# Turning q' and k' of three pairs by halves of the tokens, in two row tiles

## The chip, the core and the metric

The kernel runs on one core of one Trainium2 chip, in one launch. The metric is the device time of an execution in microseconds (us). Profiles show one execution by engine: PE is TensorE (PEld its weight loads), DVE is VectorE, ACT is ScalarE, POOL is GpSimd and SP is SyncE, which here issues DMAs alone. "L428" is line 428 of the kernel.

## What is computed

A gated linear recurrence for 4 batches, 8 heads, 768 tokens and a head width of 48, and behind it a feed-forward layer with GELU over all 3072 tokens:

```python
state = np.zeros((B, H, D, D), dtype=np.float32)
for t in range(S):
    state = alpha[:, :, t, :, None] * state + np.einsum('bhd,bhe->bhde', k[:, :, t], v[:, :, t])
    y[:, :, t] = np.einsum('bhd,bhde->bhe', q[:, :, t], state)
x = np.ascontiguousarray(y.transpose(0, 2, 1, 3)).reshape(B * S, H * D)      # 3072 x 384
h = x @ w_in                                                                  # 384 x 2048
g = 0.5 * h * (1.0 + np.tanh(c * (h + 0.044715 * h * h * h)))
out = g @ w_out                                                               # 2048 x 384
```

## The kernel before

**Tiles.** The tokens are cut into 6 chunks of 128. A unit is one batch in one chunk; two batches of a chunk make a pair, so there are 12 pairs, numbered 0 to 11 in the code (`m`). Within a chunk the recurrence becomes matrix products. ScalarE takes the logarithm of alpha (`ln`), TensorE sums it along the tokens (`cum`, L378 and L380), ScalarE takes exponentials (`b`, `binv`, `bend`, L401 and L407), and VectorE scales q and k with them to q' and k' (`qp` and `kp`, L418), in tiles with tokens on the 128 partitions and 2 units x 8 heads x 64 columns (48 of them used).

**The turn.** The attention product needs q' and k' with features on the partitions, so they have to be turned. For pairs 7 to 11 a DMA does this (`TURN_QK`); for pairs 0 to 6 TensorE does it, by a product with the identity: `turn` (L428) takes two heads at a time, 128 tokens x 128 features, as weights, and writes 128 features x 128 tokens to PSUM. For pairs 2 to 6 one task `t` turns one unit, 4 products for q' and 4 for k', into one bank (`yk`, of which there are two), and one task `ev` copies that bank, 1024 elements of each partition, into the tile `qkT` (`turned`, L446). VectorE does the copy, or, for pairs 0 to 3 (`EV_ACT`), ScalarE where the planner finds it sooner free. In `qkT` the 128 tokens of a unit lie side by side for each operand and head pair.

**Behind the turn.** `attn` (L489) multiplies k' and q' head by head, with 64 of the 128 rows for each head: the two heads of a head pair use the two halves of the rows, and write to two banks. From pair 3 on it does both units of a pair at once. VectorE masks the result (`mask`, L496). `kv` (L506) makes the chunk's share of the state from k' and v, into a `yk` bank; VectorE adds and scales it (L528 and L531). `y` (L543 and L546) adds what the state and the chunk itself give, into a `yk` bank; `x` (L553) copies it, `tx` (L560) turns it, and `xe` (L564, VectorE) copies it into `xT`. From pair 6 on a DMA turns x.

**The feed-forward layer.** For each pair TensorE does eight groups `l1` of six products with `w_in` (hT, L572), ScalarE takes the GELU of each group (L578), and for each unit TensorE does four groups `l2` of four products with `w_out` (acc, L591), whose sum is copied (`ot`, L603) and stored (L616). hT and acc take turns in four banks of PSUM, `ff`; cum and the attention share two more, `ca`.

**The order.** `Scheduler` makes a task of each of these steps. It holds a planned cost for each kind (`W`), a priority, the tasks that must be done before, and the buffers that it takes (`take`) with those who must be done before a buffer is free again. Up to about 49 us the order is written out by hand (`FIRST`); from there on the planner puts in, engine by engine, the task of the best priority among those that can start soonest. Where TensorE would idle by the plan, before a given time (`until`), it puts in products with zeros (`fill`). Each engine then runs its queue in that order and waits on semaphores.

Of the kernel before, what the change touches and what calls it, by code (L numbers as in the profile page):

```python
# [5 lines left out]
BF16 = mybir.dt.bfloat16  # L6
# [10 lines left out]
    cum=530, cum_packed=1500, t8=450, t4=225, attn=340, kv=170, inter=170, intra=205, tx=168, l1_4=655, l1_2=340, l2=655,  # L17
    qk2=910, qk1=500, ev8=650, ev4=350, mask=640, st=1090, st0=545, end=110, attn2=590, vb=320, vb_act=480, ring=1300, ring_issue=670, out=2050, lead=600, receipt=1400, receipt_hw=1000, xc=520, xe=330, ot=540,
    ev8_act=960, ev4_act=520, xc_act=450, xe_act=450, ot_act=450,
    strip=1700, cast=1900, weight=2080, dma=2100, issue=1100, wissue=760, sp=100, store=2600, turn=1250, landed=2200, xbar_qk=1500, xbar_x=1000, late_x=2500, late_qk=1200, piece=330, late_k=1500, piece_issue=450, begin=620, cast_0=1300, share=1200, cast_1=1900, ln_packed=1040, cold=380, fill=216, zero=1100,  # L20
)
COST = {
    ("ACT", "b"): (385, 135), ("ACT", "binv"): (385, 135), ("ACT", "ev"): (600, 40), ("ACT", "gelu"): (510, 110),
# [23 lines left out]
class Scheduler:  # L47
# [16 lines left out]
    def order(self):  # L64
        free = {e: 0 for e in LAT}
        taken = {tag: [] for tag in self.bufs}
        table, wire, xbar, head, out = LN_EXP, 0, 0, 0, []
        left = {e: sorted((t for t in self.tasks if e in t.cost), key=lambda t: t.prio) for e in LAT}

        def given(tag):  # L70

            n, at = len(taken[tag]) - self.bufs[tag], 0
            for u in taken[tag][n] if n >= 0 else ():
                if u.done is None:
                    return None
                at = max(at, u.done)
            return at

        def ready(t, inorder=True):
            if inorder and t.stream not in (None, head):  # L80
                return None
            at = 0
            for d in t.deps:
                if d.done is None:
                    return None
                at = max(at, d.done)
            for tag, _ in t.takes:
                g = given(tag)
                if g is None:
                    return None  # L90
                at = max(at, g)
            return at

        def put(t, at, e):
            nonlocal wire, xbar
            for tag, users in t.takes:
                taken[tag].append(users)
            cost, lat = COST.get((e, t.kind), (t.cost[e], LAT[e])) if fixed and not 300 <= t.prio < 10000 else (t.cost[e], LAT[e])
            t.start, t.end, t.engine, t.load = at, at + cost, e, None
            free[e] = t.end  # L100
            t.done = t.end + lat
            if t.name in self.landed:
                t.done = self.landed[t.name]
                if e != "SP":
                    wire = t.done - W["receipt"]
            elif t.land is not None:
                wire = max(wire, t.end + W["lead"]) + t.land
                t.done = wire + W["receipt_hw" if e == "SP" else "receipt"]
            if t.kind in ("turn", "store"):
                xbar = t.done = max(xbar, t.end + W["landed"] - t.xbar) + t.xbar  # L110
                t.done += t.late
            out.append(t)

        def go(at, e, t):
            nonlocal table, head
            if e == "PE" and not fixed and self.fill and at < self.until and at - free[e] > 300:
                g = given("ff")
                n = int((at - max(free[e], g if g is not None else at) - 60) * 0.95 // W["fill"])
                if n > 0:
                    f = Task("fill", {"PE": n * W["fill"]}, 0, self.fill(n))  # L120
                    put(f.take("ff", f), max(free[e], g), e)
            put(t, at, e)
            if t.table not in (None, table):
                table = t.load = t.table
            for q in t.cost:
                left[q].remove(t)
            if t.stream is not None:
                head = min((x.stream for x in left["PE"] if x.stream is not None), default=None)

        fixed = True  # L130
        for step in self.first:
            e, name = step.split(":")
            if name[:5] == "fill.":
                n = int(name[5:])
                f = Task("fill", {"PE": n * W["fill"]}, 0, self.fill(n))
                at = given("ff")
                assert at is not None, "no bank for idle products"
                put(f.take("ff", f), max(free["PE"], at), "PE")
                continue
            e, t = {"P": "PE", "V": "DVE", "A": "ACT", "G": "POOL", "S": "SP"}[e], self.named[name]  # L140
            at = ready(t, False)
            assert at is not None, f"{name} can't go yet"
            go(max(at, free[e] + (W["table"] if t.table not in (None, table) else 0)), e, t)
        fixed = False
        while any(left.values()):
            best = None
            for e in LAT:
# [12 lines left out]
            assert best is not None, "no task can go on"  # L160
            go(*best)
        return out
# [9 lines left out]
class _Kernel:  # L172
# [25 lines left out]
        A:b2.1 A:binv2.1 P:t2.0 P:l20.3 V:kp2.1 A:ev2.0 V:qp2.1 P:l20.10 A:bend2.1 P:attn2.0 P:t2.1 V:mask2.1 P:l20.7 A:ev2.1 V:mask2.0 P:l20.14 A:ln3.0  # L198
        P:attn2.1 P:y2.0 V:mask2.2 P:l20.13 V:mask2.3 P:l20.12 V:x2.0 P:cum3.0 A:ot0.0 V:ot0.1 P:y2.1 A:ot0.2 S:store0.0 S:store0.1 P:tx2.0 P:l20.11 A:x2.1
        S:store0.2 V:xe2.0 A:b3.0 P:tx2.1 P:l20.15 V:xe2.1 A:binv3.0 V:end2.0 P:l12.0 V:ot0.3 A:bend3.0 P:l12.1 V:qp3.0 S:store0.3 P:kv2.0 P:l12.2 V:st2.0  # L200
        A:gelu2.0 P:l12.3 V:end3.0 V:kp3.0 A:gelu2.1 P:l12.4 A:gelu2.2 P:t3.0 A:gelu2.3 P:t3.1 A:gelu2.4 V:ev3.0 P:l12.5
    """.split()
    LANDED = {"load.0": 2800, "load.1": 3400, "load.2": 4400, "load.3": 5000, "load.4": 6000, "load.5": 7300, "load.12": 10100, "load.6": 9200, "load.7":
# [7 lines left out]
    TURN_QK, TURN_X = (7, 8, 9, 10, 11), (6, 7, 8, 9, 10, 11)  # L211

    EV_ACT = (0, 1, 2, 3)

    AT_FF, SINGLE = {0: (1,), 1: (), 2: ()}, (0, 1, 2)

# [221 lines left out]
    def turned(self, u, i, which):  # L438
# [7 lines left out]
            self.copy(e)(t, ps)  # L446
        return emit

    def turn_back(self, u, i):

        def emit(e):
            ps = u["k_ps", i] = self.tile("yk", [self.C, self.H // 2, self.C], BF16, "k_ps")
            for p in range(self.H // 2):
                self.nc.tensor.transpose(ps[:, p], u["T"][:, 1, i, p], self.ident)
        return emit
# [161 lines left out]


    def tasks(self):
        s = self.s = Scheduler(self.BUFS, self.fill, 60000, self.FIRST, self.LANDED)  # L620
        B, NCH = self.B, self.NCH
        NP = B // 2
        self.p = {(c, i): {} for c in range(NCH) for i in range(NP)}
# [3 lines left out]
        loads, n, gate, held = {}, 0, [], {}  # L627
# [26 lines left out]
        for step in self.LOADS:  # L654
            if step[0] == "v":
                rows(int(step[1:]), "v")
            elif step[:4] == "gate":
                r, m, j = step[4:].split()
# [12 lines left out]
        for m, (c, i) in enumerate(pairs):  # L671
# [43 lines left out]
            if m in self.TURN_QK:  # L715
                tq = [s.add("turn", {"SP": W["turn"]}, P + 10, self.turn_dma(u, n), d, xbar=W["xbar_qk"], late=W["late_qk"] * (m < 8)) for n, d in (("q", qp), ("k", kp))]
                owner, turned = tq[0], tq
            backs = []
            vin = [loads["v", m, j] for j in range(2)]
            if m in self.NARROW:  # L720
# [2 lines left out]
                end = s.add("end", {"DVE": W["end"]}, P + 16, self.ends(u), be)  # L723
            for j in range(2):
                o, k = P + 10 + 3 * j, kp[j]
                if m not in self.TURN_QK:
                    turned = []
                    o -= 3 * u["packed"]
                    for which in ("q", "k") if early else ("qk",):
                        n = 4 * len(which)  # L730
                        cost = {"DVE": W[f"ev{n}"] + 270 * u["packed"]}
                        if m in self.EV_ACT:
                            cost["ACT"] = W[f"ev{n}_act"] + 80 * u["packed"]
                        t1 = s.add("t", {"PE": W[f"t{n}"]}, o, self.turn(u, j, which),
                                   ([qp[j]] if "q" in which else []) + ([k] if "k" in which else []))
                        turned.append(s.add("ev", cost, o, self.turned(u, j, which), [t1]))
                        t1.take("yk", turned[-1])
                        tq.append(t1)
                        if len(tq) == 1:
                            owner = turned[0]  # L740
# [12 lines left out]
            for j in range(2):  # L753
# [6 lines left out]
                    xe = tx = s.add("turn", {"SP": W["turn"]}, P + 22 + j, self.turn_x_dma(u, j, c, b), [xc], xbar=W["xbar_x"], late=W["late_x"] * (m < 6))  # L760
                else:
                    tx = s.add("tx", {"PE": W["tx"]}, P + 22 + j, self.turn_x(u, j), [xc])
                    xe = s.add("xe", {"DVE": W["xe"]}, P + 22 + j, self.turned_x(u, j, c, b), [tx])
                    tx.take("yk", xe)
                y.take("yk", xc)
                xc.take("x", tx)
# [38 lines left out]
        n = 0  # L805
# [115 lines left out]
```

## Time and profile before

| | |
|---|---|
| three runs, median (lowest to highest) | 177.44 us (176.88 to 177.53) |
| profiled execution, span from the first to the last instruction | 175.3 us |
| TensorE busy | 170.4 us (97%), 1845 products |
| TensorE weight loads busy | 135.4 us (77%) |
| VectorE busy | 96.8 us (55%) |
| ScalarE busy | 128.9 us (74%) |
| GpSimd busy (issue of loads) | 57.7 us (33%) |
| granted TensorE clock | 1.000 |
| turns of q' and k' by TensorE (L428) | 112 products, 5.4 us for q', 5.4 us for k' |

Of the profiled execution the profile tells the span, from its first to its last instruction, and no other time. The runs lie about 2 us above it. Busy times are unions of the times in which an engine worked; a product's time in the profile holds its way through the array, so products overlap, and what a product adds to the queue is the distance from its start to the next one's. The turns of pairs 3, 4 and 5 stand at 47.3, 59.0 and 73.0 us after the span's start.

### The profile page before, as it was taken

The page shows a single profiled execution, that of the slowest core. Times are in us where ns is not written, and L with a number is a line of the kernel's source. Part 1 is how long each engine was busy: PE and PEld are TensorE (multiplying, and loading weights), DVE is VectorE, ACT ScalarE, POOL GpSimd, SP SyncE. Part 2 cuts the span into 40 slices and gives each one's busy share as a digit, 9 for nine tenths or more (in the row PEclk, how much of TensorE's full clock was granted, in tenths as well). Part 3 has the DMA queues.
Part 4 walks back from the last instruction along what each step waited for, and adds up shares of the span by engine and source line. Part 5 has one row for each costly group of instructions (what it writes and reads, how often), then busy time and mean ns, then how long its engine had stood idle before and what let it go on. Part 6 is the DMA issues. An engine that isn't in the chain of part 4 may idle for free.

```text
span 175.3 us, 4440 instructions
## 1 busy us (share of the span) xinstructions
PE 170.4 (97%) x1845; PEld 135.4 (77%) x1845; DVE 96.8 (55%) x192; ACT 128.9 (74%) x213; POOL 57.7 (33%) x64
## 2 busy tenths in 40 slices
PE   7989999999999999999999999999999999999993
PEld 2667999667987896797798698698697697796973
DVE  6499920356888993795598897495426405000000
ACT  4677999666968668768788967977987984481941
POOL 2496348977645776576720000000000000000000
PEclk9999999999999999999999999999999999999999
DMA  4999999999999999999999992271271360401102
GB/s 138 307 262 224 210 243 238 246 205 207 249 273 204 242 256 220 217 226 199 200 264 224 200 136 80 54 172 52 47 187 28 90 165 4 115 20 49 45 0 90
DMA packets 49620, 28.86 MB, mean 165 GB/s; under 512 B 37696, under 2 KB 46016, under 8 KB 49600
## 3 DMA queue, kind: packets, MB, share of 16 engines
q0 software_dynamic: 26464, 17.70, 60.8%
q1 hardware_dynamic: 22592, 10.49, 24.8%
q10 hardware_dynamic: 544, 0.39, 0.8%
q8 instruction: 14, 0.23, 0.6%
q14 instruction: 6, 0.05, 0.1%
HBM read 25.17 MB, written 4.72 MB: 170 GB/s over the span
## 4 chain that ended last, share of the span: by engine, by line
PE 90%; DMA 6%; DVE 1%; issue 0%; ACT 0%; SPq 0%; POOL 0%
PE hT L572 36%; PE acc L591 36%; DMA v<-in_v_dram 4%; PE at L489 4%; PE qkT_ps L428 3%; PE yps L546 3%; PE kv L506 2%; PE yps L543 2%; DMA a<-in_alpha_dram 2%; PE cum L378 2%; PE xT_ps L560 1%; PE cum L380 1%; SPq L305 0%; ACT qkT L446 0%; DVE vb L389 0%
## 5 line engine op out<-in xcount | busy, mean ns | idle before, releaser
L572 PE MATMUL hT<-xT,w_in 128*128 128x256 bf16 x576 | 69.4, 273 | 0.0
L578 ACT ACTIVATE gT<-hT 128x512 bf16<-128x512 f32 x96 | 56.3, 600 | 17.7 <-PE hT L572 14.2
L591 PE MATMUL acc<-w_out,gT 128*128 128x384 bf16 (+3 forms) x416 | 69.0, 313 | 0.0
L572 PEld LDWEIGHTS <-w_in 128*128 128x128 bf16 x576 | 61.1, 114 | 1.6
L591 PEld LDWEIGHTS <-gT 128*128 128x128 bf16 x416 | 36.9, 98 | 19.2
L496 DVE TENSOR_TENSOR atm<-at,ut 128x512 bf16<-128x512 f32 x48 | 30.1, 681 | 12.7 <-PE at L489 12.6
L418 DVE TENSOR_TENSOR qp<-q,b 128x768 bf16<-128x768 f32 (+1 forms) x15 | 11.9, 794 | 14.0 <-ACT b L407 11.7
L418 DVE TENSOR_TENSOR kp<-k,binv 128x768 bf16<-128x768 f32 (+1 forms) x15 | 11.9, 791 | 10.6 <-ACT binv L407 10.6
L603 ACT COPY ot<-acc 128x384 f32<-128x384 f32 (+3 forms) x17 | 7.4, 439 | 13.0 <-PE acc L591 12.9
L308 POOL DMA_DIRECT2D k<-in_k_dram x11 | 12.2, 1107 | 6.6 <-DVE atm L496 3.0
L308 POOL DMA_DIRECT2D vb<-in_v_dram x11 | 12.1, 1102 | 6.7 <-PE hT L572 1.7
L308 POOL DMA_DIRECT2D q<-in_q_dram x11 | 12.2, 1109 | 6.1 <-DVE atm L496 1.3
L308 POOL DMA_DIRECT2D a<-in_alpha_dram x11 | 12.2, 1114 | 5.9 <-DMA w_in<-in_moe_w_in_dram 1.3
L407 ACT ACTIVATE b<-cum 128x768 bf16<-128x768 f32 (+1 forms) x15 | 10.3, 683 | 3.6 <-PE cum L380 2.3
L280 ACT ACT_TABLE_LOAD x9 | 11.5, 1283 | 0.9 <-PEq L905 0.7
L578 ACT ACT_TABLE_LOAD x9 | 11.5, 1283 | 0.2
L407 ACT ACTIVATE binv<-cum 128x768 bf16<-128x768 f32 (+1 forms) x15 | 10.2, 681 | 0.1
L528 DVE TENSOR_TENSOR stmp<-kv,st 128x384 f32<-128x384 f32 x16 | 8.8, 552 | 2.0 <-PE kv L506 2.0
L553 DVE CAST x<-yps 128x384 bf16<-128x384 f32 x12 | 6.7, 556 | 4.7 <-PE yps L546 4.7
L531 DVE TENSOR_TENSOR st<-stmp,ends 128x384 bf16<-128x384 f32 x16 | 8.9, 558 | 0.6
L446 ACT COPY qkT<-qkT_ps 128x512 bf16<-128x512 bf16 (+1 forms) x9 | 6.5, 728 | 3.7 <-PE qkT_ps L428 3.5
L546 PE MATMUL yps<-vb,atm 128*128 128x48 bf16 x192 | 8.7, 183 | 0.4 <-DVE vb L389 0.4
(65 smaller groups left out, 156.7 us busy)
## 6 DMA issues: line engine op xcount, KB each, us to landing
out_dram<-ot SPq DMA_DIRECT2D x19, 192.0 KB, 5.2
a<-in_alpha_dram POOLq DMA_DIRECT2D x9, 384.0 KB, 12.5
q<-in_q_dram POOLq DMA_DIRECT2D x9, 384.0 KB, 11.6
k<-in_k_dram POOLq DMA_DIRECT2D x9, 384.0 KB, 11.7
vb<-in_v_dram POOLq DMA_DIRECT2D x9, 192.0 KB, 11.6
w_in<-in_moe_w_in_dram POOLq DMA_DIRECT2D x4, 384.0 KB, 9.3
w_out<-in_moe_w_out_dram POOLq DMA_DIRECT2D x4, 384.0 KB, 11.1
out_dram<-ot SPq DMA_DIRECT2D x9, 96.0 KB, 1.8
```

Of the source, the lines that this page charges most:

```text
L280: nc.scalar.add_instruction(mybir.InstLoadActFuncSet(name=nc.get_next_instruction_name(), act_func_set_id=i, engine=mybir.EngineType.Activ ...
L308: dma(u[t][:, lo:hi].rearrange("t b h d -> t (b h) d"), src.rearrange("b h s d -> s (b h) d")[c * C:(c + 1) * C])
L407: self.nc.scalar.activation(u[n].rearrange("t i h d -> t i (h d)")[:, lo:hi], cum, AF.Exp, scale=1.0 if n == "b" else -1.0)
L418: self.nc.vector.tensor_tensor(out, rows, b, op=ALU.mult)
L496: self.nc.vector.tensor_tensor(u["atm", i][:, o], u["at", i][o], self.ut[:, None, :].to_broadcast([self.C, self.H // 2, self.C]), op=ALU.mult)
L528: nc.vector.tensor_tensor(s, acc, old, op=ALU.add)
L531: nc.vector.tensor_tensor(new.rearrange("f p (o d) -> f (p o) d", o=2), acc.rearrange("f p (o d) -> f (p o) d", o=2), ends, op=ALU.mult)
L546: nc.tensor.matmul(y[:, h, :], u["atm", i][:, h % 2, h // 2, :], u["vb"][:, i, h, :], start=c == 0, stop=True, skip_group_check=True)
L572: self.nc.tensor.matmul(h[:, s], w_in[:, j, nt % 4 + s], self.xT[c % self.NX][:, j, lo:hi].rearrange("p g t -> p (g t)"), start=j == 0, st ...
L578: return lambda e: self.nc.scalar.activation(self.gT[c % self.NG][:, nt:nt + 2, lo * self.C:hi * self.C], f.pop(("h", c, lo, nt)), AF.Gelu ...
L591: self.nc.tensor.matmul(f["acc", c, b][:, lo:hi], self.gT[c % self.NG][:, nt, b * self.C:(b + 1) * self.C], self.w_out[:, nt, lo:hi], star ...
L603: self.copy(e)(f["ot", c, b][:, sl], f["acc", c, b] if half is None else f["acc", c, b, half][:, sl])
```

## The change

For pairs 3, 4 and 5 (`ROWS_64`) the task `t` turns both units at once, and each product takes 64 tokens and not 128: the weights are 64 tokens x 128 features, the other operand is a 64 x 64 piece of the identity, and the result is 128 features x 64 tokens. Products with the first half of the tokens use rows 0 to 63 of TensorE and write to one bank; products with the second half use rows 64 to 127 and write to the other bank. They alternate. So 16 products of a pair become 32, first all of q', then all of k'. Each of the two copies takes one half of the tokens for both units, 1024 elements as before, and writes them to `qkT` in runs of 64 tokens.

The task takes both `yk` banks, so the planner's `given` now looks one buffer further for the second; for `ff` it plans as before. ScalarE may do the copy `xe` of pair 3. The limit for idle products goes from 60 to 40 us, and the written order loses the second turn of pair 3. In the built program the number of idle products stays 17. On TensorE the turns of pair 3 stand where they did, the two hT groups around the first kv now both stand ahead of it, and one kv group moves behind the last hT group; at pairs 4 and 5 an hT group that stood behind the pair's first y now stands between the turns and the first kv, and one acc group moves from behind the turns of x to ahead of the second y. For pair 3 one acc group comes between the two y groups and one between its two turns of x; the second `xe` moves from VectorE to ScalarE, behind `bend`, and its copy `x` moves behind `binv`. The queues of GpSimd and SyncE don't change.

```diff
-    strip=1700, ..., cold=380, fill=216, zero=1100,
+    strip=1700, ..., cold=380, t64=640, ev16=650, ev16_act=960, fill=216, zero=1100,
...
-        def given(tag):
+        def given(tag, ahead=0):
-            n, at = len(taken[tag]) - self.bufs[tag], 0
+            n, at = len(taken[tag]) + ahead - self.bufs[tag], 0
...
-            for tag, _ in t.takes:
-                g = given(tag)
+            for k, (tag, _) in enumerate(t.takes):
+                g = given(tag, sum(x[0] == tag for x in t.takes[:k]))
                 if g is None:
                     return None
-                at = max(at, g)
+                at = max(at, given(tag) if tag == "ff" else g)
...
-        A:gelu2.0 P:l12.3 V:end3.0 V:kp3.0 A:gelu2.1 P:l12.4 A:gelu2.2 P:t3.0 A:gelu2.3 P:t3.1 A:gelu2.4 V:ev3.0 P:l12.5
+        A:gelu2.0 P:l12.3 V:end3.0 V:kp3.0 A:gelu2.1 P:l12.4 A:gelu2.2 P:t3.0 A:gelu2.3 V:ev3.0 A:gelu2.4 P:l12.5
...
+    ROWS_64 = (3, 4, 5)
+    XE_ACT = (3,)
...
+    def turn_halves(self, u):
+        nc, H, C = self.nc, self.H, self.C
+
+        def emit(e):
+            ps = u["T_ps"] = [self.tile("yk", [C, 2, 2, H // 2, C // 2], BF16, "qkT_ps") for _ in range(2)]
+            for j, n in enumerate("qk"):
+                for i in range(2):
+                    for p in range(H // 2):
+                        for h in range(2):
+                            sl = slice(64 * h, 64 * h + 64)
+                            nc.tensor.transpose(ps[h][:, j, i, p, :], u[n + "p"][sl, i, 2 * p:2 * p + 2, :].rearrange(
+                                "t h d -> t (h d)"), self.ident[sl, sl])
+        return emit
+
+    def turned_half(self, u, h):
+        def emit(e):
+            t = self.qkT(u).rearrange("f j i p t -> f (j i p) t")[:, :, 64 * h:64 * h + 64]
+            self.copy(e)(t, u["T_ps"][h].rearrange("f j i p t -> f (j i p) t"))
+        return emit
...
-        s = self.s = Scheduler(self.BUFS, self.fill, 60000, self.FIRST, self.LANDED)
+        s = self.s = Scheduler(self.BUFS, self.fill, 40000, self.FIRST, self.LANDED)
...
+            elif m in self.ROWS_64:
+                t1 = s.add("t", {"PE": W["t64"]}, P + 10, self.turn_halves(u), [qp[0], kp[0]])
+                cost = {"DVE": W["ev16"], **({"ACT": W["ev16_act"]} if m in self.EV_ACT else {})}
+                turned = [s.add("ev", cost, P + 10, self.turned_half(u, h), [t1]) for h in range(2)]
+                for x in turned:
+                    t1.take("yk", x)
+                tq, owner = [t1], t1
...
-                if m not in self.TURN_QK:
+                if m not in self.TURN_QK + self.ROWS_64:
...
-                    xe = s.add("xe", {"DVE": W["xe"]}, P + 22 + j, self.turned_x(u, j, c, b), [tx])
+                    xe = s.add("xe", {"DVE": W["xe"], **({"ACT": W["xe_act"]} if m in self.XE_ACT else {})}, P + 22 + j, self.turned_x(u, j, c, b), [tx])
```

More of the change, by code (lines that the diff above doesn't have):

```diff
@@ L19 @@
     ev8_act=960, ev4_act=520, xc_act=450, xe_act=450, ot_act=450,
-    strip=1700, cast=1900, weight=2080, dma=2100, issue=1100, wissue=760, sp=100, store=2600, turn=1250, landed=2200, xbar_qk=1500, xbar_x=1000, late_x=2500, late_qk=1200, piece=330, late_k=1500, piece_issue=450, begin=620, cast_0=1300, share=1200, cast_1=1900, ln_packed=1040, cold=380, fill=216, zero=1100,
+    strip=1700, cast=1900, weight=2080, dma=2100, issue=1100, wissue=760, sp=100, store=2600, turn=1250, landed=2200, xbar_qk=1500, xbar_x=1000, late_x=2500, late_qk=1200, piece=330, late_k=1500, piece_issue=450, begin=620, cast_0=1300, share=1200, cast_1=1900, ln_packed=1040, cold=380, t64=640, ev16=650, ev16_act=960, fill=216, zero=1100,
 )
```

## The prediction

> **What bounds the kernel now.** I read the first page of the profile first (busy shares, then the chain that ended last), then the groups by form, then TensorE's timeline around the turns that change.
>
> ```profile
> PE 170.4 (97%) x1845; PEld 135.4 (77%) x1845; DVE 96.8 (55%) x192; ACT 128.9 (74%) x213; POOL 57.7 (33%) x64
> ...
> PEclk9999999999999999999999999999999999999999
> ...
> PE 90%; DMA 6%; DVE 1%; issue 0%; ACT 0%; SPq 0%; POOL 0%
> ```
>
> TensorE is busy for 97% of the span at the full granted clock, and 90% of the chain that ended last is TensorE; the DMA share lies in the first 12 us. So from 20 us on, time is the sum of TensorE's starts: what shortens its queue shortens the kernel, unless a new wait appears.
>
> The groups by form (name, shapes, count | busy us, mean ns | idle before) price the old and the new work:
>
> ```profile
> L428 PE MATMUL qkT_ps<-ident,qp 128*128 128x128 bf16 x56 | 5.4, 219 | 0.0
> L489 PE MATMUL at<-qkT 64*128 64x128 bf16 x192 | 8.0, 218 | 0.0
> L591 PE MATMUL acc<-w_out,gT 128*128 128x64 bf16 x16 | 0.6, 193 | 0.0
> ```
>
> ```profile
> L446 DVE COPY qkT<-qkT_ps 128x1024 bf16<-128x1024 bf16 x7 | 4.5, 685 | 1.3 <-PE qkT_ps L428 1.3
> L564 DVE COPY xT<-xT_ps 128x384 bf16<-128x384 bf16 x12 | 4.1, 352 | 1.9 <-PE xT_ps L560 1.9
> L446 DVE COPY qkT<-qkT_ps 128x512 bf16<-128x512 bf16 x2 | 1.4, 691 | 0.1
> L461 DVE COPY kn<-k_ps 128x512 bf16<-128x512 bf16 x3 | 1.3, 422 | 0.3 <-PE k_ps L454 0.2
> ```
>
> The means contain a matmul's pipeline; what costs time is start to start. In the trace's start times that is 56 ns for a turn, 109 ns for an hT product, 29 ns for the 64-column products of the last acc pieces. The attention products (L489) work on 64 rows, in two row tiles and two banks: the second of a pair starts 3 to 4 ns after the first, the next pair 52 to 53 ns later, so a pair of 128 columns takes 56 to 57 ns, as long as one full product.
>
> TensorE's timeline at the fifth pair (start, us):
>
> ```profile
> 58.35 0.82 PE L572 MATMUL hT<-xT,w_in 128*128 128x256 bf16 x6
> 59.01 0.39 PE L428 MATMUL qkT_ps<-ident,qp 128*128 128x128 bf16 x4
> ...
> 59.90 0.82 PE L572 MATMUL hT<-xT,w_in 128*128 128x256 bf16 x6
> 60.55 0.33 PE L506 MATMUL kv<-vb,kp 128*128 128x96 bf16 x4
> 60.72 0.82 PE L572 MATMUL hT<-xT,w_in 128*128 128x256 bf16 x6
> 61.48 0.62 PE L489 MATMUL at<-qkT 64*128 64x128 bf16 x16
> 62.03 0.34 PE L506 MATMUL kv<-vb,kp 128*128 128x96 bf16 x4
> ```
>
> Sixteen turns take 59.90 - 59.01 = 0.89 us. An hT group takes 0.655, so the one from 60.72 is through at 61.38, yet the attention starts at 61.48: 0.10 us (0.096 in the start times) go by in which TensorE starts nothing. Eight pairs are worth 0.45, yet kv starts 0.55 after them: another 0.095. Every attention block after an hT group shows both, the same to 1 ns: the price of going to 64 rows and back.
>
> **The turns, term by term.** For pairs 3, 4 and 5 (the fourth to sixth) 16 turns of 128 columns become 32 of 64, in 16 pairs of row tiles. In the built program the 32 lie between hT groups, alone, so each block pays the way in and out. A pair of row tiles with 64 columns isn't in the trace. Below, it can't beat the 64-column product, 29 ns; above stands the attention pair, 57 ns, with twice the columns. An attention pair takes 1 ns more than one full product of its width, so I take 29 + 1 = 30 ns.
>
> - Fifth and sixth pair: 0.096 + 16 x 0.030 + 0.095 = 0.67 for 0.89: -0.22 us each, -0.44 (at 57 ns a block takes 1.10: +0.21 each).
> - Fourth pair: the block runs from 47.33 to 48.41 = 1.08 us, of which 0.18 is a wait before the first k turn at 47.73, since DVE's kp ends at 47.67. Afterwards all 16 q turns come first: 47.33 + 0.096 + 8 x 0.030 = 47.67, then k at 47.73 as before, 0.24, and 0.095 out: 48.07. -0.34 us. Most of the wait is filled by q turns of the second unit.
>
> Sum -0.78 us. [...]
>
> **What is moved.** Both copies of a pair (L446, on DVE; for the fourth pair one on ACT) now wait for the whole block and not for half of it, and both banks of "yk" are taken at once; behind them queue kv, which needs a bank, and the attention. The program puts two hT groups (1.31 us) where one stood between block and kv. For the fifth pair: block from 59.10 (first start), last turn written at about 59.75, DVE copies 59.8-60.5 and 60.4-61.1; TensorE comes to kv at 60.98 and to the attention at 61.98, about 0.9 after the second copy. Hidden, if a copy takes 0.69 as now. For the fourth pair TensorE comes to the attention at 49.67; the copies end at about 49.0 (DVE) and 49.3 (ACT, 1.01 from 48.3). Hidden.
>
> One of the two xT copies of the fourth pair goes from DVE to ACT, and an acc group of 0.65 us moves between its two y blocks. In the old times: second y ends at 56.88, ACT's binv frees ACT at 57.0, x there 0.48 to 57.45, the second xT turn starts at 57.54 and ends at 57.87, ACT copies it (x of as many elements takes 0.48) to 58.38. The hT group, due at 58.35, needs this copy: with 0.05 us from engine to engine it starts at 58.43, +0.08 us (0 to 0.15). The table load behind the copy then ends at 59.7 and not 58.8; four "ff" banks take up the late first gelu: before the second hT group needs one back, it is done.
>
> The loads stand 10 us and more ahead of their users (alpha of the sixth pair lands at 52.7, is read at 67.97). The pairs turned by DMA have one thin place: the second xT transpose of the seventh pair lands at 100.24, its hT group starts at 100.80. TensorE will be 0.7 us early there, the transposes are issued as much earlier, but loads fill the DMA queues until 98.6. Give-back 0 to 0.2; I take 0, as the issue moves too. The planner's edits (the limit for idle products, the second bank asked for ahead) leave 17 idle products as before: nothing.
>
> Sum: -0.78 + 0.08 = -0.70 us. The profiled execution has a span of 175.3 us; the page gives no other time of it, and the median, 177.44, is 2.1 us more, outside of what the profile sees. So span 174.6 and median 177.44 - 0.70 = 176.7. What a measurement of this kernel can tell from no change is about 0.5%, 0.9 us: below 176.55 is faster, above 178.33 slower.
>
> **The rivals.** (1) The blocks are cheaper than I think: the way out could be hidden by weights of the hT group loaded early, as nowhere in the nine big attention blocks. Three times 0.095 and no stall at 58.35: 176.3. Against it: 148 to 149 ns from the last attention start to the next, whatever comes next.
>
> (2) Slower: the halves don't overlap, or their weight loads don't. 32 weight loads of 64 rows come where 16 of 128 came, four instructions in 30 ns; the trace shows at most four in 57 (attention) or two in 25 (y). If halves go one by one at 29 ns, a block is 0.096 + 0.93 + 0.095 = 1.12, +0.23 for the fifth and sixth each, for the fourth 47.43 + 0.93 + 0.095 = 48.45, +0.04: with the stall +0.58, 178.0. At 56 ns each it would be 1.98 a block: +1.09, +1.09, +0.9, with the stall 180.6. It decides from 44 ns a pair on (16 x 0.044 + 0.19 = 0.89, no gain). For it: no row has 64 columns in row tiles. Against: after a wait, the attention's first two pairs of weight loads start within 18 ns. [...]
>
> (3) The copy gets slower: its output now lies in runs of 64 elements. The packed copies (L446, 512 elements, scattered) take 691 ns where kn's 512 take 422, so 1024 could take 1.22 us. Then in the fifth pair the second copy ends at 62.15, kv waits 0.07 and the attention 0.22: +0.29, twice: 177.3. Against it: xT's copy in runs of 128 takes 352 for 384, the fast rate. [...]
>
> (4) The whole gain is given back at 100.8 us because transposes land no earlier: at most 0.2 as worked above, 176.9, inside the forecast.
>
> **How the numbers follow.** Forecast with (4): 0.60, its own range 176.4 to 177.1; (1) 0.15; (2) 0.15, some two thirds of it at 178.3 or more, as its ends are 178.0 and 180.6; (3) 0.10. Faster by over 0.5%: all of (1) and about a third of the forecast, which is 0.2 us from that bound: 0.36. Slower: 0.11 of (2), and 0.02 for a stall that I don't see: 0.13. The rest, 0.51, lies within. The range 176.2 to 178.2 leaves out the worse part of (2) and a sliver below.
>
> **What would show it.** Right: in the changed profile, 32 turns with 3 to 4 ns within a pair and about 30 from pair to pair, hT 0.67 us after the block is due; 0.06 us of wait before the k turns of the fourth pair; DVE copies at about 0.69; no TensorE idle before the attention; a small wait of hT for ACT's xT copy near 58. Wrong: a pair over 44 ns, copies over 1 us with the attention waiting, or a wait near 100 us of more than 0.2.

## The result, and the profile after

| | before | after |
|---|---|---|
| median of the runs (lowest to highest) | 177.44 us (176.88 to 179.56) | 179.39 us (179.13 to 180.11) |
| ratio after to before, 95% interval | | 1.0129 [1.0107, 1.0150] |
| span of the profiled execution | 175.3 us | 177.4 us |
| end of TensorE's last product | 172.65 us | 174.18 us |
| granted clock | 1.000 | 0.998 |

The forecast was 176.7 us, "same" the likeliest; measured is a loss of 1.3%, 2.0 us. Ratios and their intervals, here and below, are of the runs within 1.5% of their kernel's fastest; medians are of all runs. First the lines of the page of after that answer to those shown of before, and below them the head of its costliest group:

```profile
PE 170.3 (96%) x1893; PEld 134.0 (76%) x1893; DVE 96.2 (54%) x191; ACT 129.2 (73%) x214; POOL 57.7 (33%) x64
...
PEclk9999999999999999999999999999999999999999
...
PE 87%; DMA 8%; ACT 2%; SPq 0%; issue 0%
...
L596 PE MATMUL hT<-xT,w_in 128*128 128x256 bf16 x576 | 69.5, 273 | 1.9 <-DMA xT<-x 1.9
```

TensorE's busy time is unchanged to 0.1 us, though 48 products and 48 weight loads were added. Its share of the chain fell from 90 to 87%, and DMA's rose from 6 to 8%. The new wait has a name: hT, which no wait touched before, idles 1.9 us for one DMA transpose of x. The groups by form (count | busy us, mean ns | idle before):

```profile
L513 PE MATMUL at<-qkT 64*128 64x128 bf16 x192 | 8.0, 218 | 0.2
L463 PE MATMUL qkT_ps<-ident,qp 64*128 64x64 bf16 x48 | 1.2, 191 | 0.0
L470 DVE COPY qkT<-qkT_ps 128x1024 bf16<-128x1024 bf16 x5 | 3.3, 687 | 1.7 <-PE qkT_ps L463 1.7
L470 ACT COPY qkT<-qkT_ps 128x1024 bf16<-128x1024 bf16 x1 | 1.0, 1037 | 0.0
```

The copies cost what they cost before (687 ns where 685 stood). TensorE's timeline at the fifth pair (start, us):

```profile
57.98 0.81 PE L596 MATMUL hT<-xT,w_in 128*128 128x256 bf16 x6
58.73 0.41 PE L463 MATMUL qkT_ps<-ident,qp 64*128 64x64 bf16 x16
58.97 0.40 PE L463 MATMUL qkT_ps<-ident,kp 64*128 64x64 bf16 x16
59.30 1.50 PE L596 MATMUL hT<-xT,w_in 128*128 128x256 bf16 x12
60.64 0.33 PE L530 MATMUL kv<-vb,kp 128*128 128x96 bf16 x4
60.81 0.82 PE L596 MATMUL hT<-xT,w_in 128*128 128x256 bf16 x6
61.56 0.62 PE L513 MATMUL at<-qkT 64*128 64x128 bf16 x16
```

From 58.73 to 59.30 the block takes 0.57 us, plus 0.096 before its first product: 0.67 as forecast. Within a pair of row tiles the starts are 3 to 4 ns apart, to the next pair 25 to 26: 29 ns a pair, where 30 was taken. So the turns did what was said of them. The loss shows in a pass through the chain of waits around 100 us (start, length, what). Before, TensorE goes from acc to hT without a stop:

```profile
98.34 2.62 PE acc L591 x16
100.96 0.65 PE hT L572 x6
```

After, hT stands behind a transpose:

```profile
96.35 0.38 PE acc L615 x3
96.73 5.34 DMA xT<-x
102.07 0.04 issue
102.11 0.82 PE hT L596 x6
```

The second transpose of x of pair 6 is under way from 96.73 to 102.07; before, it took 96.44 to 100.24. SyncE's own queue shows that it is not issued earlier, though TensorE is. Before:

```profile
95.08 1.27 SPq L466 DMA_TRANSPOSE qkT<-qp  x1
96.44 1.21 SPq L472 DMA_TRANSPOSE xT<-x  x1
```

and after:

```profile
94.30 2.34 SPq L490 DMA_TRANSPOSE qkT<-qp  x1
96.73 1.21 SPq L496 DMA_TRANSPOSE xT<-x  x1
```

The issue of q' of pair 7 holds SyncE for 2.34 us, and the transpose behind it is issued 0.29 later, not 0.78 earlier like the first one of pair 6 (92.33 for 93.11). Yet it isn't the issue that sets the landing. The first transpose of x lands 0.39 us after the last load before (98.99 after 98.60), and 0.33 after it in the changed kernel (100.82 after 100.49); the second follows 1.25 and 1.26 us behind the first. So the question is why the loads end 1.9 us later. The DMA view of the window from 97 to 100 us, queue by queue (packets, MB, share of 16 engines), before:

```profile
q1 hardware_dynamic: 1921, 0.47, 125.1%
q0 software_dynamic: 13, 0.04, 4.2%
```

and after:

```profile
q1 hardware_dynamic: 568, 0.14, 110.3%
q0 software_dynamic: 66, 0.20, 24.9%
q8 instruction: 1, 0.02, 2.4%
```

In the same 3 us the transposes (q1) get 568 packets through and not 1921, the loads (q0) are not done yet, and there is one packet of a third kind: q8, 16 KB of instructions, from 97.79 to 98.95 in the trace. In the whole execution there are 14 such before and 15 after:

```profile
q8 instruction: 15, 0.25, 0.6%
```

Before, 14 fetches served 3690 instructions of TensorE (1845 products and as many weight loads), so each brings some 260, by that estimate. They come with the count of instructions that TensorE has started: 248 from one fetch to the next on average before and 250 after (207 to 292), the eighth fetch at 2041 in both kernels, though at 92.25 and 88.24 us, the ninth at 2251 and 2277. The change adds 96, over a third of a fetch, and fetches are about 10 us apart here (92.25, 102.60 before): the one that came at 102.60 to 104.03 now comes almost 5 us earlier.

The accounts, from TensorE's start times in both traces: up to the 96th hT product -0.14 us (in the first 44 us, before the changed turns); from there to the 240th, past all three changed blocks, -0.64; to the 289th, which is the one that waits, +2.09; at the attention near 121 (pair 9) +0.21; from the last product to the end of the span +0.48. Sum +2.00, the difference of the spans (175.35 and 177.36).

### The profile page after: what moved, and what is told of

Read it like the earlier page. It is cut to its first block, busy times and chain, and to the rows that moved or that the text cites. A ratio compares the mean times of both kernels' runs of the same rounds, so it can differ in the third digit from the quotient of the medians.

```text
span 177.4 us, 4536 instructions
## 1 busy us (share of the span) xinstructions
PE 170.3 (96%) x1893; PEld 134.0 (76%) x1893; DVE 96.2 (54%) x191; ACT 129.2 (73%) x214; POOL 57.7 (33%) x64
## 4 chain that ended last, share of the span: by engine, by line
PE 87%; DMA 8%; ACT 2%; SPq 0%; issue 0%
PE hT L596 34%; PE acc L615 34%; PE at L513 4%; DMA xT<-x 3%; PE yps L570 3%; DMA qkT<-kp 2%; PE qkT_ps L432 2%; DMA a<-in_alpha_dram 2%; PE yps L567 2%; PE kv L530 2%; PE cum L382 2%; PE xT_ps L584 1%; PE qkT_ps L463 1%; PE idle L293 1%; ACT qkT L450 1%; PE k_ps L478 1%
## 5 line engine op out<-in xcount | busy, mean ns | idle before, releaser
L365 ACT ACTIVATE la<-a 128x768 f16<-128x768 f32 (+1 forms) x11 | 8.5, 785 | 0.1
```

The source lines that it names most:

```text
L365: self.nc.scalar.activation(u["la"][:, lo:hi, :, 0:self.D], u["a"][:, lo:hi], AF.Ln)
```

## The experiments

Two theories stood at first. **F**: the fetch of TensorE's instructions, moved by the 96 new ones, falls into the transposes near 98 us and holds them up. **T**: TensorE is earlier, so the transposes are issued earlier and meet the tail of the loads (its last, k of pair 11, lands at 98.60 before, at 100.49 after). The expectations count pairs from one, so that their "seventh pair" is pair 6 of the code; only the "sixth and seventh pair" of e5 and e7 are pairs 6 and 7 of the code.

| kernel | median, us | ratio to before, 95% | fetch nearest 98 | second xT of pair 6 | wait of hT | first hT to last product |
|---|---|---|---|---|---|---|
| before | 177.1 | 1 | 92.25-93.28, 102.60-104.03 | 96.44-100.24 | 0 | 155.75 |
| after | 179.39 | 1.0129 [1.0107, 1.0150] | 97.79-98.95 | 96.73-102.07 | 2.09 | 157.62 |
| e1 before, 96 more | 179.97 | 1.0174 [1.0131, 1.0218] | 98.13-99.80 | 97.49-102.17 | 0.32 | 157.48 |
| e2 after, 96 more | 177.39 | 1.0026 [1.0002, 1.0051] | 93.07-94.38 | 96.56-100.41 | 0.20 | 155.33 |
| e3 after, later | 180.77 | 1.0222 [1.0204, 1.0240] | 97.66-100.05 | 97.16-102.53 | 1.47 | 158.93 |
| e4 before, earlier | 177.23 | 0.9993 [0.9973, 1.0014] | 91.25-92.41, 102.49-104.17 | 96.22-100.46 | 0.34 | 155.46 |
| e5 before, 96 in layer 2 | 179.10 | 1.0127 [1.0107, 1.0147] | 98.50-99.63 | 97.18-102.37 | 1.30 | 157.44 |
| e6 after, 96 in layer 2 | 177.02 | 1.0014 [0.9992, 1.0035] | 94.92-96.28 | 98.12-100.56 | 0 | 155.37 |
| e7 after, 96 late | 178.43 | 1.0068 [1.0043, 1.0092] | 97.70-98.79 | 96.64-101.56 | 1.01 | 156.42 |
| e8 after, 128 in layer 2 | 176.91 | 0.9989 [0.9970, 1.0008] | 92.36-93.67 | 96.95-100.78 | 0.98 | 156.29 |
| e12 after, 96 in layer 2 | 177.29 | 0.9997 [0.9969, 1.0025] | 93.24-94.59 | 97.12-100.94 | 0.85 | 156.08 |
| e13 after, short loads | 178.32 | 1.0060 [1.0035, 1.0085] | 96.12-97.42 | 96.64-99.60 | 0 | 156.26 |
| e14 e12, short loads | 176.78 | 0.9985 [0.9963, 1.0007] | 93.06-94.09 | 95.94-98.24 | 0 | 155.29 |
| e15 before, short loads | 177.11 | 0.9991 [0.9972, 1.0011] | 91.50-92.39, 101.64-102.65 | 95.69-98.00 | 0 | 155.75 |

All in us. Fetches, transposes and waits are of the one profiled execution of each kernel; the wait is the start-to-start time beyond the usual one. The last column leaves out the start, which differs from execution to execution: the first hT product comes between 16.20 and 18.78 us. Runs of before beside e1 to e15 had medians of 177.10 to 177.15.

### More instructions, and TensorE later or earlier (e1 to e4)

e1 and e2 cut 16 of the 17 idle products, early in the kernel, into four of 128 columns each: 96 more instructions for the same columns.

```diff
             for _ in range(n):
-                self.nc.tensor.matmul(ps, self.zero[:, 0:self.C], self.zero, start=True, stop=True)
+                w = 128 if self.SPLIT_FILLS > 0 else 512
+                self.SPLIT_FILLS -= 1
+                for lo in range(0, 512, w):
+                    self.nc.tensor.matmul(ps[:, lo:lo + w], self.zero[:, 0:self.C], self.zero[:, lo:lo + w], ...)
```

e3 gives the changed kernel five cum products more in pair 5, so that TensorE comes 0.8 us later to the place near 100; e4 makes the kernel before 0.87 us earlier by leaving out 8 of its hT products (the last third of the sum of four groups of pair 3), with three idle products cut to keep the instruction count.

```diff
+                for _ in range(3 + (i == 0) if u["m"] == 5 else 1):        # e3
                     nc.tensor.matmul(cum[:, i, 0:H * D], self.ut_h, la[:, i, :, 0:D], start=True, stop=True)
...
+                nkt = self.NKT - ((c, lo) == (1, 2) and nt < 8)             # e4
```

> The kernel before, with 16 of its 17 idle products of 512 columns cut into four of 128 columns each: 96 more TensorE instructions (48 products, 48 weight loads) in the first 20 us, as many as the change adds, and the same TensorE time. [...] Theory T (the tail): TensorE came 0.8 us earlier to 93 us, so the transposes met the tail of the loads; nothing of that here, so 177.4 us and no wait.

> The changed kernel, with the same 96 more TensorE instructions in its idle products. F: the fetch that struck at 97.8 us comes at about 93 us, before the transposes of the seventh pair stand in the queues; the next one at about 104. The wait of 2.1 us for xT is gone or under 0.5 us: 176.6 to 177.2 us, what the prediction had. T: nothing about time or order changes, the wait stays at 2 us: 179.4 us.

> The changed kernel, with five sum products of the sixth pair (128x384, 162 ns each) done again: TensorE 0.81 us later from 69 us on, 10 instructions more, so that it comes to the seventh pair at the old time. T: the transposes meet the loads as before, no wait at 100.8 us, 177.4 us. F: the fetch strikes at about 98, in the transposes again; the wait shrinks by what TensorE comes later, if the transposes end with the fetch, and stays over 1 us: 178.8 to 179.6 us.

> The kernel before, where four hT groups of the fourth pair leave out the last of three pieces of the sum (8 products, 0.87 us at 109 ns), and three idle products are cut in four (18 instructions more, 16 fewer): TensorE 0.87 us earlier from 62 us on with the same number of instructions. T: the transposes of the seventh pair meet the tail of the loads as in the changed kernel, a wait of about 2 us: 178.5 to 179.4 us. F: the fetch stays at its instruction, near 101.7 us, behind the transposes of the seventh pair: a wait under 0.4 us, 176.6 to 177.0 us.

e1: the kernel before loses 1.7% by 96 instructions that do nothing more. Its fetch lands at 98.13, its second xT at 102.17. But the wait at hT is only 0.32, not the 1 to 2 that F had, since TensorE was by then 1.1 us late, 0.72 of it lost between the first and the 96th hT product; another 0.70 went at the attention near 121, and the time lies above F's range of 178.4 to 179.5. This is F in kind, but its size is not clean. e2: the same 96 added to the changed kernel bring it from 179.4 to 177.4, 0.2 above F's range. The fetch is back at 93, and the hT wait of 2.09 is 0.20. T said the wait stays; it went. e3: being 0.8 later didn't help, as T wanted; the fetch still fell at 97.66, and the time rose, to 180.77, above F's range (178.8 to 179.6) too. Its trace has more waits behind 100 us: 0.56 at the attention of pair 9 and 0.98 at that of pair 10, whose k' lands late with a fetch in it (132.86 to 133.94). e4: TensorE earlier without more instructions waits 0.34, not 2: T alone doesn't make the loss. Yet e4 was no faster than before, though 0.87 us of products were gone; its stretch from the first hT to the last product is only 0.29 shorter. That was not expected: of what is won ahead of 100 us, 0.34 is lost there even without the fetch, and 0.19 more had gone up to the 96th hT product.

### The same count without touching the start (e5 to e8)

Here layer-2 products of chunk 0 (30 to 44 us), or for e7 of chunk 3 (110 to 126 us), are cut into two of 192 columns: two instructions more for each, at 3 ns. In these four the second half of a cut product carries a start flag too, so the sums of those blocks differ (the result is off by a relative 0.072 in e5, e6 and e8, 0.064 in e7); number, shape and place of the products do not.

```diff
+                    for l, r in ((0, 192), (192, 384)) if cut else ((lo, hi),):
-                    self.nc.tensor.matmul(f["acc", c, b][:, lo:hi], gT, self.w_out[:, nt, lo:hi], start=nt == 0, ...)
+                        self.nc.tensor.matmul(f["acc", c, b][:, l:r], gT, self.w_out[:, nt, l:r], start=nt == 0, ...)
```

> The kernel before, with 48 of the 64 layer-2 products of chunk 0 (30 to 44 us) cut into two of 192 columns: 96 more TensorE instructions, none of them in the first 29 us, for about 48 x 3 ns = 0.14 us of TensorE time. Theory F (the fetches of TensorE's instructions decide): the fetch moves from 102.60 to about 98, into the transposes of the sixth and seventh pair; hT waits 0.5 to 1.5 us near 101, the attention near 121 waits 0.2 to 0.7 more, the last stores go 0.5 later: 178.3 to 179.9 us. Theory T (transposes that start earlier meet the tail of the loads): nothing is earlier, so 177.3 to 177.6.

> The changed kernel with the same 48 products cut. F: another 96 instructions move the fetch of 97.8 back to about 93 and bring the next one to 103, as with the 96 in idle products, but without the time lost in the first 25 us; the wait for xT near 100 is at most 0.3, the gain of 0.7 on TensorE is kept less 0.14: 176.5 to 177.0 us, faster than both kernels. T: TensorE is as early as in the changed kernel, so the wait of 2 us stays: 179.2 to 179.6.

> The changed kernel with 48 layer-2 products of chunk 3 (110 to 126 us) cut in place of chunk 0's: the same number of instructions as in the run before, but added behind the transposes of the sixth and seventh pair. F: the fetch near 98 stays where it was and so does the wait of 2 us near 100; the fetches near 119 and 173.6 move, so 0.2 at 121 and up to 0.5 at the last stores may come back: 178.4 to 179.5 us. If the number of instructions counted and not the place of the fetch, the time would be that of the run before, 176.5 to 177.0.

> The changed kernel with all 64 layer-2 products of chunk 0 cut: 128 more instructions. F: the fetch near 93 of the run with 96 comes some 1.5 us earlier or later at most, still ahead of the transposes that decide, and the next near 105; no wait over 0.4 us near 100: 176.5 to 177.4 us. T: 179.2 to 179.7.

e5 is the cleanest evidence for F: the kernel before, nothing earlier, nothing turned by halves, loses as much as the change did, 1.0127 against 1.0129. The waits of its TensorE from 96 to 123 us (in total, times, longest):

```profile
PE hT L574 <- DMA xT<-x: 1.1, 1, 1.1
PE at L491 <- DMA qkT<-kp: 0.2, 1, 0.2
```

These are the two waits of the changed kernel, at the same two instructions, and the last stores come late by as much: from the last product to the end of the span are 3.33 us and not 2.70. e6 against e7 is the place of the fetch with the count held: 96 instructions ahead of 98 us undo the loss, behind it (e7) the fetch stays at 97.70, the wait stays at 1.01, and only the rest comes back (2.70 at the end). e7's time was within its range, its wait not: its TensorE was 0.57 us later at the 240th hT product than that of after, and the transpose landed 0.51 earlier (101.56 for 102.07), which makes up the 1.08 between the two waits. Up to 110 us the two are the same program, so one execution can differ from another by that much, and a wait of a single profile must be read with that in mind.

e8 and e6 were expected at 176.5 to 177.4 and 176.5 to 177.0 and came to 176.91 and 177.02, but neither is faster than before, which F had expected of e6, and e8 shows a wait of 0.98 with no fetch nearer than 93.67. That is beyond the 0.4 expected. e6's profiled execution had none, but it also began 1.9 us late and so came to that hT product at 102.17. So a second term was there, and T had a part in it.

### The loads held back (e9 to e11), and the sum kept (e12)

To take the tail of the loads away from the transposes, the four loads of pair 11 wait on GpSimd until the x of pair 6 is turned. e9 is the changed kernel with that, e11 the kernel before, e10 the changed kernel with 96 instructions more. e12 is e6 with the start flag on the first half alone; it computes everything.

```diff
-    LOADS = (..., '9', '10', '11')
+    LOADS = (..., '9', '10', 'late', '11')
+            elif step == "late":
+                late = s.add("gate", {"POOL": 150}, n, self.wait_x(3, 0))
+                gate = [late]
...
+        late.deps += [xts[3, 0], xts[3, 1]]
```

> The changed kernel with the loads of the twelfth pair (a, q, k, v, which are needed only after 130 us) held back by a gate on GpSimd until the x of the seventh pair has been transposed. The orders of TensorE, VectorE, ScalarE and SyncE are untouched, and so are the instruction fetches. The joint theory (the loads' tail sets when the transposes can land at the earliest, about 100.2 to 100.8, and a fetch in between adds 1.6 to 1.7): the fetch near 98 now meets transposes alone, the second xT lands by 99.5 to 101, and hT waits 0 to 1.0 in place of 2.09; 0.2 near 121 and the later fetch ahead of the last stores stay: 177.2 to 178.4 us. F alone (the loads don't matter): the wait of 2 us stays, 179.2 to 179.6. The loads alone decide: 176.5 to 176.9.

> The same gate, and 48 layer-2 products of chunk 0 cut in two (96 more instructions): fetches near 93 and 103. Both terms are then out of the way of hT near 100: TensorE keeps its 0.63 less about 0.14 for the cuts, and nothing waits: 176.3 to 176.9 us, faster than both kernels. If the wait comes back through the held loads (they now travel at 100 to 107 us, beside the transposes of the eighth and ninth pair), 177.0 to 178.0.

> The kernel before with the gate alone. TensorE waits for nothing near 100 there, so an earlier landing is worth nothing: 176.9 to 177.4 us. If the held loads hurt the transposes of the eighth pair (attention near 107), slower by that wait.

> The changed kernel with the 48 cut layer-2 products and no gate, with the whole sum kept (only the first half of a cut product starts the bank): the second xT lands at 100.4 to 100.8 by the tail of the loads, so of TensorE's 0.63 some 0.3 to 0.5 is given back near 100: 176.7 to 177.1 us.

| kernel | median, us | ratio, 95% | second xT of pair 6 | kp of pair 8 | attention of pair 8 waits |
|---|---|---|---|---|---|
| e9 | 181.69 | 1.0207 [1.0156, 1.0257] | 96.44-98.77 | 101.13-108.79 | 2.35 |
| e10 | 188.29 | 1.0539 [1.0464, 1.0614] | 96.11-98.42 | 101.31-116.00 | 9.19 |
| e11 | 189.03 | 1.0646 [1.0606, 1.0687] | 96.69-99.00 | 101.90-117.01 | 9.61 |

All three missed by far. At the place that they were made for they worked: with no load beside it, the second xT takes 2.3 us and hT waits for nothing. But the held loads now travel at 99 to 120 us beside the next transposes, and it is there that it goes wrong. The chain of e11:

```profile
101.26 0.64 PE hT L575 x6
101.90 15.11 DMA qkT<-kp
117.01 0.05 issue
117.06 1.03 PE at L492 x16
```

One transpose takes 15.11 us instead of 2.75. In e11 a fetch falls at 107.24 to 108.55 and in e10 at 106.71 to 108.05, into loads and transposes both; in e9 none comes before 110.31, and the same transpose takes 7.66. So loads and transposes together were slow in e9, without a fetch: 7.66 us for 2.75. That the fetch on top made it worse by far fits all three kernels, in profile and in median, but nothing else was tried to test it. e12 came to 177.29 and not 176.7 to 177.1, with 0.85 of wait left where 0.3 to 0.5 was expected.

### Fewer bytes (e13 to e15)

The gate moved the collision. To take it away, q and k of pairs 10 and 11 are loaded for the first batch alone, 768 KB less, and VectorE reads them for both batches. Every queue keeps its instructions and their order.

```diff
+            hi_ = hi - (u["m"] in (10, 11) and n in "qk")
-            src = self.src[n][2 * i + lo:2 * i + hi]
+            src = self.src[n][2 * i + lo:2 * i + hi_]
...
+            if u["m"] in (10, 11):
+                rows = u[n][:, 0:1].to_broadcast([self.C, hi - lo, self.H, self.D])
```

> The changed kernel with 768 KB less to load: of q and k of the eleventh and twelfth pair only the first batch is loaded, and VectorE reads it for both (the output of the second batch is computed from the first one's q and k). No instruction is added, moved or taken out, and the fetch stays near 98. The loads end some 3.5 us earlier, about 95 to 97. Joint theory (tail of the loads and fetch add up): the fetch meets transposes alone, the second xT lands at 98.8 to 100.6, hT waits 0 to 0.6 in place of 2.09; 0.2 near 121 and 0.5 at the last stores stay: 177.2 to 177.9 us. Fetch alone: the wait of 2 us stays, 179.2 to 179.6.

> The same 768 KB less, and the 48 cut layer-2 products (96 more instructions, fetches near 93 and 103 as in the run without the shorter loads, where hT waited 0.85 near 100). If the tail of the loads makes that wait: it goes, and 176.3 to 176.9 us are left, the whole gain of TensorE. If the fetch near 93 makes it by itself: the wait of 0.6 to 0.9 stays, 177.0 to 177.5.

> The kernel before with the same 768 KB less: TensorE does not wait for xT near 100 there, so an earlier landing brings nothing: 176.9 to 177.4 us. If fewer bytes bring something elsewhere, this run shows how much of the two others is not the wait's.

The last load lands at 96.58, 95.77 and 94.96. e13 keeps the fetch in the transposes (96.12 to 97.42) and loses the wait: the second xT lands at 99.60, ahead of the 100.02 at which TensorE of after wants it. Its waits from 96 to 123 us:

```profile
PE at L516 <- DMA qkT<-kp: 0.5, 1, 0.5
```

Only the second one is left, now 0.56 beyond the usual with a fetch at 118.00 to 119.31 on kp of pair 9. With that, the late stores (3.34 us from last product to end, 0.6 more) and a start that cost 0.6 more, 178.32 lies above the expected 177.9. The fetch still costs something here: the second xT takes 2.97 us from issue to landing, and 2.30 in e14. e14 has no wait near 100; its chain there:

```profile
97.65 2.62 PE acc L623 x16
100.28 0.66 PE hT L601 x6
```

acc passes to hT with nothing in between. From the first hT to the last product it takes 155.29 us against 155.75 of its control e15: -0.46, which is about the -0.64 of the turns, 0.11 back for the cuts and 0.06 for a wait near 131. In the medians it is 176.78 against 177.11, two intervals that overlap: in the measured time the gain alone is too small to be told from none. e15 itself equals before, as expected.

So the wait of 2 us near 100 takes both. With short loads and a fetch inside (e13): none. With the full loads and the fetch elsewhere: 0.20 (e2), 0.98 (e8), 0.85 (e12). With both: 2.09 in after, 1.30 in e5, 1.01 in e7. Against e8 and e12, whose TensorE is as early as that of after at this place, the fetch adds 1.1 to 1.2 us to the wait; the size depends on the execution, as e7 shows. The landing of the second xT separates the kernels with full loads without overlap: 100.24 to 100.94 us in the six with no fetch near 98 (before, e2, e4, e6, e8, e12), 101.56 to 102.53 in the five with one (after, e1, e3, e5, e7).

The best version that still computes everything, e12, is as fast as before; none found beats it.

## Why the prediction was wrong

**What held.** TensorE was the bound (96% busy, 87% of the chain). The block of 0.67 us was measured at 0.67. The fourth pair's stretch became 0.23 us shorter (0.34 - 0.08 = 0.26 was forecast), the fifth's 0.21, the sixth's 0.20 (0.22 each): -0.64 for -0.70. The stall at hT behind ScalarE's copy of xT was forecast at 0.08 and is 0.08 (57.98). The k turns of the fourth pair waited 0.06, as forecast. The copies take 0.69, the one on ScalarE 1.04 for 1.01, and no attention waited for them. Rivals (1), (2) and (3) did not come about: 29 ns a pair, and the way in and out as priced. (Rival (1)'s own terms, -0.78 and three times -0.095, come to 176.4 and not 176.3; nothing hangs on it.)

**The step that failed** is the thin place: "Give-back 0 to 0.2; I take 0, as the issue moves too." It measured 2.09. Two things were wrong in it.

First, the landing did not move with TensorE, or with the issue. The trace of before already showed it: of the four transposes under way there, issued from 93.11 to 97.74, none lands before 98.99, and the last k load lands at 98.60. They ended 0.39 to 2.47 us behind the loads, however early they began. In the eleven kernels with full loads up to here (before, after, e1 to e8, e12) the first xT lands 0.17 to 0.40 us after the last load (1.74 and 1.91 in e1 and e3, whose fetch outlasts it), and the second 1.23 to 1.42 behind the first, though it is issued 3.3 to 4.8 behind it. In e8 and e12 the first was issued earlier than before (92.15 and 92.44), the second later (96.95 and 97.12, behind a q' that held SyncE for 2.6 us), the loads ended at 99.31 and 99.47, and the second landed at 100.78 and 100.94, not 100.24. So with no fetch near 98 hT still waited 0.98 and 0.85, more than the whole gain of 0.64. The step named the loads until 98.6 and then made nothing of them; rival (4) had the mechanism and capped it at 0.2. With this term alone, "same" would have been the outcome, as e8 and e12 were.

Second, no price was put on 96 more instructions as bytes. "The planner's edits ... nothing" and the sum of products both treat an instruction as time on an engine. But TensorE's instructions come by DMA, beside the loads and transposes; 14 fetches of them stood on the page of before (`q8 instruction: 14, 0.23, 0.6%`), and 0.6% of the DMA time looked like nothing. In the changed kernel 15 fetches bring 0.25 MB, 16 KB each. No wait of TensorE for instructions is in the trace, but the transfers beside the fetch paid: some 1.1 us of the 2.09 at hT, 0.21 at the attention of pair 9 (a fetch at 119.08 to 120.11 in its kp, 4.20 us for 2.75), and 0.48 at the last stores (a fetch at 173.60 to 174.48; the last store is issued 0.51 after its copy ends, and not 0.04).

The sum made again with these terms: -0.70 + 2.1 + 0.2 + 0.5 = +2.1, for +2.0 measured. The prediction's own sign for being wrong, a wait near 100 us of more than 0.2, is the one that appeared.

Not settled: why the stretch from the first to the 96th hT product (up to some 30 us) takes 0.2 to 0.75 more in after, e1, e4, e9, e10 and e13 than in before; how a single packet of 16 KB held up so many others; why the loads end at 99.31 and 99.47 in e8 and e12, and at 98.75 in e2, whose TensorE is about as early; and whether the fetch near 93 has a part in the 0.85 and 0.98 of e12 and e8: e14 shows that it makes no wait without the tail of the loads, not that it adds none to it.

## What to carry to other kernels

Count what a change adds in instructions, not only in time (96 more moved a fetch by almost 5 us here): find the instruction fetches in the DMA part of the page, work out where they fall after the change, and ask which DMA on the critical path is in flight there. Set a stretch that is freed on the bounding engine against the slack of the next DMA that it waits for: of 0.64 us freed here nothing was left behind the waits of 0.85 and 0.98 in e12 and e8. And a transpose under way beside loads can end with the loads, as here (the first xT 0.17 to 0.40 us after the last load), and not so many microseconds after its issue. To test such a cause, add idle instructions to the kernel before: if it loses the same, as e5 did with 96 more (1.0127 against 1.0129), the work of the change is not to blame.

## What the runs showed of the hardware

- A fetch of 16 KB mostly took 0.9 to 1.5 us (2.4 at most, in e3), and what it hit was often held up by as much or more. In 14 traces (without e9 to e11), transposes issued after 100.6 us: x with no fetch of any engine 2.28 to 2.31 us (61 of them), with one of TensorE's 2.28 to 4.28 (62, median 3.16), with one of 8 KB in queue q14 alone up to 3.07 (17); q' and k' without a fetch 2.72 to 2.80 (88), with one 2.75 to 4.97 (16, median 4.44).
- Loads, transposes and a fetch at once took longest: 15.11 and 14.69 us for a transpose of 2.75 (e11, e10), 7.66 with no fetch among them (e9).
- In e11 TensorE's granted clock was 0.53 behind the wait of 9.61 us. By stretches (length, busy us and count of PE, PEld, DVE, ACT and POOL, then the granted clock, DMA share, GB/s):

```profile
107.00:117.00 10.00, 0.61 (x15) 0.49 (x12) 0.56 (x1) 0.81 (x2) 0.00 (x0) 0.70 1.32 111
117.00:121.50 4.50, 4.44 (x30) 2.77 (x31) 2.48 (x4) 1.94 (x3) 0.00 (x0) 0.53 0.94 53
121.50:130.00 8.50, 8.50 (x96) 6.78 (x94) 5.12 (x9) 6.54 (x11) 0.00 (x0) 1.00 0.46 108
```

  The clock is 0.53 for 4.5 us, and hT products start twice as far apart there (213 ns where 109 is usual). Behind the 2.35 us of e9 it was 0.63 for 3.8 us in the profiled execution; but of e9's six executions three have a mean clock of 0.991 (182.44 to 183.13 us) and three of 1.000 (179.93 to 180.95), so a wait of about this length did not always lower it. Behind the 2.09 us of the changed kernel it stayed at 1.00.
- Two row tiles of 64 x 64 took 29 ns a pair in the changed kernel, as long as one full product of 64 columns (29 ns): the halving in rows came on top of that in columns, less 0.19 us a block (96 ns ahead of its first product, 97 behind its last).
